# Half of V computed in the opening, half between later attention units

## The chip, the cores and the metric

One core of a Trainium2 chip runs the whole program. The metric is the device time of one execution in microseconds. TensorE (PE) does the matmuls and loads their weights on a parallel path (PEld); VectorE (DVE), ScalarE (ACT) and GpSimd (POOL) do the element-wise work; SyncE (SP) and GpSimd issue most of the transfers.

## What is computed

Forward and backward of a transformer block with modulation, B = 1, S = 2048, D = 512, F = 1792, 32 heads of 16 columns. The change touches only the forward of the attention, cut here from the reference:

```python
mod = (_silu(c) @ w_mod).reshape(c.shape[0], 6, 1, -1)
h = _layernorm(x, axis=-1) * (1 + ca) + sa
qkv = (h @ wqkv).reshape(B, S, 3, H, Dh).transpose(2, 0, 3, 1, 4)
q, k, v = qkv[0], qkv[1], qkv[2]
scores = einsum('bhqd,bhkd->bhqk', q, k) * Dh ** -0.5
o = einsum('bhqk,bhkd->bhqd', softmax(scores), v)
x = x + ga * (o.transpose(0, 2, 1, 3).reshape(B, S, D) @ wo)
```

An MLP with a squared ReLU follows, and the gradients of all of it with respect to nine inputs.

## The kernel before

**Forward attention.** The queries are cut into 4 chunks of 512 (`qc`), the heads into 8 groups of four (`g`), and each group into two halves of two heads (`jp`). A step `n` is one (qc, g, jp); n = 0 to 15 are the first chunk, and pair g is n = 2g and 2g + 1. A step has 16 units, one for each block of 128 keys (`kb`). A unit is: two score matmuls of 512 columns (one for each head), one exponential of 128x1024 on ACT from PSUM to `pu`, and, two or more units later, eight P·V matmuls of 17 columns, which use blocks of `pu` as weights and `Vaug` (V with a column of ones) as the moving operand. Score tiles `st` have two buffers. The score matmul takes all 128 rows: `QTm[j]` holds one head's Q in its 32 rows and zeros elsewhere, and KTq holds the K of the four heads of a group.

**The opening.** `gen_open` loads x, normalises it in four blocks of 512 tokens, transposes and modulates it into `xm1T`, and computes, per block, the K of pair 0 and V (`value`, L517 to L522: four matmuls of 512 columns per 128 tokens, all 32 heads, copied to `Vaug` by DVE or ACT). The first 32 units (n = 0 and 1, exponential L357) run between these pieces: one `next(first)` advances the opening by one piece per unit, so that one unit holds a `value`, or half a block's transposes, or the four matmuls of a Q or K block.

**The background.** From n = 2 on the exponential is L391, and a `Background` object puts other PE work between units. A generator yields after each matmul what it costs (1 for a 512-column projection matmul); each unit grants 1.2 of credit in the first chunk. `gen_qkv` is that generator: for each g from 1 to 7 it waits until the attention is at pair g - 1, then makes, with `gen_fm` (four matmuls, a DVE cast to `ev_fm` or the K tile, a store to `QTq_d` or `KTq_d`), the Q of pair g for the first chunk, then its K in four blocks, then some smaller work (`gen_mod` at g = 2, `gen_vt` at g = 3 to 6, which lets eight units go by while POOL and SP make V's transposes), then the Q of pair g - 1 for the three later chunks. A block that `gen_fm` made is also transposed (L646, on SP) and kept token-major: K's by a POOL store (L648), Q's by a POOL copy (L651) and a POOL store (L653). `ev_fm`, `ev_tm` and `ev_tmc` have three buffers each; the PSUM tile `pps` has two.

**What sets the order.** PE's and SP's instructions are written out by hand in this order. POOL's are placed by the scheduler in the first chunk. Two deadlines force background work: at kb = 5 of the second step of a pair, `bg.until(g + 1)` runs the background until the next pair's Q is done, and `load_q` (L302) loads it into `QTm` through POOL's queue; at the end of that step `bg.until(-(g + 1))` runs it until the next pair's K is done. Work forced so stands in one run on PE, ahead of the next unit's scores. At the end of the first chunk `bg.drain()` finishes the rest, and the tiles of this phase are closed.

```python
for kb in range(ST):
    if kb == (5 if qc == 0 and jp == 1 else 1) and n + 1 < len(order):
        if n < 2 * NQ - 1 and jp == 1:
            bg.until(g + 1)
        load_q(*order[n + 1])
```

Of the kernel before, what the change touches and what calls it, by code (L numbers as in the profile page):

```python
# [10 lines left out]
F32 = mybir.dt.float32  # L11
# [8 lines left out]
P = 128  # L20
DH = 16
# [84 lines left out]
class K:  # L106
# [319 lines left out]
    def gen_open(self, Vaug, KT, QTm, QTo, stp, bg):  # L426

        tc, nc, io = self.tc, self.nc, self.io
        S, D, H, NQ, ST, DT, SC = self.S, self.D, self.H, self.NQ, self.ST, self.DT, self.SC
# [5 lines left out]
        xm1T = self.xm1T = sb.tile([P, DT, S], BF16, name="xm1T")  # L435
        wq = self.wq = sb.tile([P, DT, 3 * D], BF16, name="wqkv")
# [80 lines left out]
        def value(st):  # L517
            pt = ps.tile([P, 512], F32, name="pps")
            for kt in range(DT):
                nc.tensor.matmul(pt[:], lhsT=xm1T[:, kt, st * P:(st + 1) * P], rhs=wq[:, kt, 2 * D:3 * D],  # L520
                                 start=(kt == 0), stop=(kt == DT - 1))
            (nc.scalar.copy if st % 4 == 3 or st in (0, 2) else nc.vector.tensor_copy)(Vaug[:, st, :, 0:DH], pt[:].rearrange("p (h d) -> p h d", d=DH))  # L522

        def pad0(t):
            nc.scalar.copy(self.wpad0[t][:].rearrange("p k (j e) -> p k j e", e=32)[:, :, :, 0:DH],
# [54 lines left out]
        for s4 in range(0, ST, 4):  # L580
# [3 lines left out]
            for k in range(3):  # L584
                value(s4 + k)
                if not last and k in (late, late + 1):
                    norm(n4 + 2 * (k - late))
                    norm(n4 + 2 * (k - late) + 1)
                    if k > late:
                        store(n4)  # L590
                yield 0
            if s4 == 0:
                value(s4 + 3)
                pad(0)
                yield 0
# [3 lines left out]
            if s4:  # L599
                value(s4 + 3)  # L600
                yield 0
# [60 lines left out]
    def gen_qkv(self, kp):  # L662

        nc = self.nc
        S, NQ, ST = self.S, self.NQ, self.ST
        for g in range(1, NQ):
            while self.cur_g < g - 1:
                yield ("wait", 0)
            KT = self.KT_next = kp.tile([P, S], BF16, name="KTq")
            yield from self.gen_fm(self.mps, 0, g, 0)  # L670
            yield (g, 0)
            for s0 in range(0, S, 512):
                yield from self.gen_fm(self.mps, 1, g, s0, dst=KT[:, s0:s0 + 512])
            yield (-g, 0)
            if 3 < g <= 3 + self.DT:
                wt = self.qkv_eb.tile([P, 3 * self.DT, P], BF16, name="wm_t", bufs=1)
                nc.sync.dma_start_transpose(wt[:], w[:])
                nc.gpsimd.dma_start(self.WmT_d[g - 4], wt[:].rearrange("p n k -> p (n k)"))
            if 2 < g < 3 + self.DT:
                w = self.qkv_eb.tile([P, 3 * self.D], BF16, name="wm_s", bufs=2)  # L680
                sc = self.qkv_eb.tile([P, 1], F32, name="wm_c", bufs=2)
                nc.vector.tensor_copy(sc[:], self.opcaT[:, g - 3:g - 2])
                nc.gpsimd.tensor_scalar(w[:], self.wq[:, g - 3, :], sc[:], 1.0, ALU.mult, ALU.mult)
            if g == 2:
                yield from self.gen_mod()
            elif 3 <= g < 3 + self.SC:
                yield from self.gen_vt(4 * (g - 3))
            for s0 in range(512, S, 512):
                yield from self.gen_fm(self.mps, 0, g - 1, s0)
        for s0 in range(512, S, 512):  # L690
            yield from self.gen_fm(self.mps, 0, NQ - 1, s0)

    def gen_vt(self, s0):

        nc = self.nc
        NQ = self.NQ
        vT = self.qkv_eb.tile([P, NQ, 4 * P], BF16, name="vT", bufs=1)
        for k in range(4):
            vp = self.vpads[k]
            v = self.Vaug[:, s0 + k, :, 0:DH].rearrange("p (g j) d -> p g j d", j=4)  # L700
            one = self.qkv_eb.tile([P, 1], F32, name="one", bufs=2)
            nc.vector.memset(one[:], 1.0)
            nc.gpsimd.tensor_scalar(vp[:, :, 0:2, 0:DH], v[:, :, 2:4, :], one[:], 1.0, ALU.mult, ALU.mult)
            nc.gpsimd.tensor_scalar(vp[:, :, 2:4, 0:DH], v[:, :, 0:2, :], one[:], 1.0, ALU.mult, ALU.mult)
            nc.sync.dma_start_transpose(vT[:, :, k * P:(k + 1) * P], vp[:].rearrange("p g j e -> p (g j e)"))
            yield ("wait", 1)
        nc.gpsimd.dma_start(self.VTq_d.rearrange("g p s -> p g s")[:, :, s0 * P:(s0 + 4) * P], vT[:])
# [1258 lines left out]
```

## Time and profile before

| | us |
|---|---|
| median of 3 runs (2507.37 to 2510.71) | 2508.8 |
| the profiled execution's own time | 2500.32 |
| its span | 2498.5 |
| busy in the span: PE, ACT, DVE, POOL | 2410.2, 2283.1, 1695.0, 753.5 |
| opening's units (first exponential L357 to first L391) | 16.73 to 64.19 |
| pairs 1 to 3, first chunk | 64.19 to 153.45 |
| pairs 4 to 6, first chunk | 153.45 to 242.97 |
| pair 7, first chunk | 242.97 to 272.24 |

The profile is of one execution, so its rows add up to its span and not to the median. A row of the page's groups and of the timeline has the line, the engine, the operation, what it writes and reads, the shape, and how many of them (x). In the timeline the first two columns are start and length in microseconds, and a bracket tells how long the engine was idle before it and what ended that. PE's matmuls are pipelined: each row's length includes a fixed delay to its end, so what a matmul costs is read from the distance of the starts. The queue of SP is a row of issues; a long issue is one that was held up.

The granted TensorE clock is 1.00 in every stretch from 0 to 600 us that was looked at.

### The profile page before, as it was taken

The numbers are of one execution on the slowest core, as the hardware profiler recorded it, in microseconds if no ns is written. First come the engines' busy times: TensorE is split into PE (matmuls) and PEld (weight loads), VectorE is DVE, ScalarE is ACT, GpSimd is POOL, SyncE is SP. The second block draws the span as 40 slices with busy tenths as digits, with TensorE's granted clock in tenths as the row PEclk, the third lists the DMA queues.
The fourth block names the chain that finished last, engine by engine and source line by source line (L and its number), as shares of the span: only waits on it lengthen the run. The fifth ranks groups of instructions, "written<-read, shape, count | busy, mean of one in ns | idle before, by whom it ended". The sixth has DMA issues, their size and how long they took to land.

```text
span 2498.5 us, 67897 instructions
## 1 busy us (share of the span) xinstructions
PE 2410.2 (96%) x26211; PEld 1061.6 (42%) x26439; DVE 1695.0 (68%) x3487; ACT 2283.1 (91%) x3757; POOL 753.5 (30%) x1337
## 2 busy tenths in 40 slices
PE   8999999999999999999999999999999999999998
PEld 4555555555555555583233332333333333333343
DVE  6222322422332343576999999999999999999957
ACT  7999999999999997534999999999999999999945
POOL 2344531220131022245222323322333222322223
PEclk9999999999999999999999999999999999999999
DMA  4589661541243045499999999999999999999997
GB/s 166 135 179 208 169 125 47 132 100 40 92 114 98 23 123 147 110 199 216 232 235 233 232 227 231 237 234 231 230 235 239 234 230 236 234 233 236 238 217 192
DMA packets 1293547, 454.13 MB, mean 182 GB/s; under 512 B 1236948, under 2 KB 1261398, under 8 KB 1293222
## 3 DMA queue, kind: packets, MB, share of 16 engines
q1 hardware_dynamic: 1252422, 344.68, 71.8%
q0 software_dynamic: 38720, 104.04, 13.9%
q8 instruction: 207, 3.39, 0.6%
q10 hardware_dynamic: 2080, 1.05, 0.2%
q14 instruction: 118, 0.97, 0.1%
HBM read 75.83 MB, written 64.49 MB: 56 GB/s over the span
## 4 chain that ended last, share of the span: by engine, by line
PE 49%; ACT 35%; DMA 7%; issue 5%; DVE 3%; POOL 1%; SPq 1%; ACTq 0%; DVEq 0%; POOLq 0%
ACT pu L391 26%; PE st L1608 17%; PE acckv L1459 8%; ACT pu L1611 6%; DMA dsT<-ds 5%; PE accq L1484 5%; PE st L388 4%; PE dp L1522 2%; PE accbank L322 2%; PE dps L1050 2%; PE dp L1659 1%; PE st L1754 1%; ACT csq L1540 1%; PE pps L1237 1%; DVE ds L1526 1%
## 5 line engine op out<-in xcount | busy, mean ns | idle before, releaser
L1526 DVE TENSOR_TENSOR ds<-dp,pu 128x512 bf16<-128x512 f32 x1888 | 1166.0, 682 | 34.6 <-PE dp L1522 19.1
L1611 ACT ACTIVATE pu<-st 128x512 bf16<-128x512 f32 x2048 | 1073.8, 666 | 34.7 <-PE st L1608 21.3
L391 ACT ACTIVATE pu<-st 128x1024 bf16<-128x1024 f32 x992 | 912.1, 1077 | 4.2 <-PE st L388 3.7
L388 PE MATMUL st<-QTm,KTq 128*128 128x512 bf16 x1859 | 560.9, 377 | 27.1 <-ACT pu L391 6.1
L322 PEld LDWEIGHTS <-pu 128*128 128x128 bf16 x8192 | 346.7, 96 | 236.1 <-issue 3.0
L1522 PE MATMUL dp<-kvm,q 64*128 64x512 bf16 x1024 | 365.0, 384 | 2.0 <-DVE ds L1526 0.7
L322 PE MATMUL accbank<-Vaug,pu 128*128 128x17 bf16 x8192 | 357.4, 171 | 8.3 <-ACT Vaug L522 1.1
L1522 PE MATMUL dp<-kvm,dOTg 64*128 64x512 bf16 x1024 | 363.6, 383 | 0.3
L1608 PE MATMUL st<-kvm,q 64*128 64x512 bf16 x1024 | 349.4, 382 | 5.4 <-ACT pu L1611 0.2
L1608 PE MATMUL st<-kvm,QTg 64*128 64x512 bf16 x1024 | 348.1, 381 | 6.5
L1541 POOL TENSOR_TENSOR ds<-csq,pu 128x512 bf16<-128x512 f32 x128 | 147.2, 1150 | 627.0 <-ACT csq L1540 553.6
L388 PEld LDWEIGHTS <-KTq 128*128 128x128 bf16 x1984 | 188.4, 96 | 176.9 <-issue 124.8
L1459 PE MATMUL acckv<-ds,Qg 128*16 128x512 bf16 x1024 | 176.2, 382 | 0.3
L1459 PE MATMUL acckv<-pu,q 128*16 128x512 bf16 x1024 | 176.3, 383 | 0.0
L1459 PE MATMUL acckv<-ds,q 128*16 128x512 bf16 x1024 | 176.2, 383 | 0.0
L1459 PE MATMUL acckv<-pu,dOg 128*16 128x512 bf16 x1024 | 176.0, 382 | 0.0
L302 POOL DMA_DIRECT2D QTm<-QTq_d x124 | 63.1, 511 | 341.5 <-PE st L388 320.0
L1608 PEld LDWEIGHTS <-q 64*128 64x128 bf16 x1024 | 67.0, 94 | 163.5 <-issue 150.6
L1608 PEld LDWEIGHTS <-QTg 64*128 64x128 bf16 x1024 | 67.1, 94 | 160.6 <-issue 145.7
L329 DVE RECIPROCAL rl<-accbank 128x4 f32<-128x4 f32 x128 | 22.9, 179 | 158.3 <-PE accbank L322 158.2
L1522 PEld LDWEIGHTS <-q 64*128 64x128 bf16 x1024 | 88.8, 93 | 52.9 <-issue 43.3
L1522 PEld LDWEIGHTS <-dOTg 64*128 64x128 bf16 x1024 | 88.2, 93 | 52.9 <-issue 43.8
(390 smaller groups left out, 3055.1 us busy)
## 6 DMA issues: line engine op xcount, KB each, us to landing
KTq<-KTq_d POOLq DMA_DIRECT2D x24, 512.0 KB, 3.9
duT_d<-auT POOLq DMA_DIRECT2D x3, 1792.0 KB, 7.9
aT_d<-rT POOLq DMA_DIRECT2D x3, 1792.0 KB, 11.5
KTq_d<-KTq SPq DMA_DIRECT2D x32, 128.0 KB, 2.1
QTq_d<-ev_fm SPq DMA_DIRECT2D x32, 128.0 KB, 4.3
ktm_d<-ev_tm POOLq DMA_DIRECT2D x32, 128.0 KB, 2.5
VTq_d<-vT POOLq DMA_DIRECT2D x4, 1024.0 KB, 6.3
dx<-dx_d SPq DMA_DIRECT2D x16, 256.0 KB, 4.6
```

What stands on the lines that cost most here:

```text
L302: nc.gpsimd.dma_start(QTm[j][32 * j:32 * j + 32, :], self.QTq_d[g, 32 * j:32 * j + 32, 512 * qc:512 * (qc + 1)])
L322: nc.tensor.matmul(acc[:, a, sub, :], lhsT=pu[:, a, sub * P:(sub + 1) * P], rhs=Vaug[:, kb, h, :], start=(kb == 0 and a == 0 and sub == 0) ...
L388: nc.tensor.matmul(stt[:, a, :], lhsT=KT[:, kb * P:(kb + 1) * P], rhs=QTm[2 * jp + a][:], start=True, stop=True)
L391: nc.scalar.activation(pu[:], stt[:], ACT.Exp, scale=self.scale)
L1050: nc.tensor.matmul(pt[:], lhsT=a[st], rhs=g_tm[:, st, :], start=(st == 0), stop=(st == ST - 1))
L1459: nc.tensor.matmul(acckv[r:r + DH, :], lhsT=T[n][:, ib, col:col + DH], rhs=src[:, a, :], start=(ib == 0), stop=(ib == ST - 1))
L1484: nc.tensor.matmul(accq[r:r + 32, o:o + 256], lhsT=T["K"][:, 4 * c + sub, col:col + 32], rhs=v[:, r // 32 % 2 * 2:r // 32 % 2 * 2 + 2, 4 * ...
L1522: nc.tensor.matmul(dp[:], lhsT=T["dOT"][rd, ib * P:(ib + 1) * P], rhs=masked["VT"][a][rd, 512 * c:512 * (c + 1)], start=True, stop=True)
L1526: nc.vector.tensor_tensor(dsg[:, i, a], dp[:], pu[:, a, :], ALU.mult)
L1541: nc.gpsimd.tensor_tensor(dsg[:, i, 1], f[:], pu[:, 1, :], ALU.mult)
L1608: nc.tensor.matmul(stt[:], lhsT=T["QT"][rs, q], rhs=masked["KT"][a][rs, c0:c0 + 512], start=True, stop=True)
L1611: nc.scalar.activation(pu[:, a, :], stt[:], ACT.Exp, scale=self.scale)
```

## The change

`value` computes the first 256 columns of V only, that is heads 0 to 15 (pairs 0 to 3). A new generator `gen_v` computes the other 256 in the background, for token blocks 0 to 3 after the K of pair 1, 4 to 9 after that of pair 2, and 10 to 15 after that of pair 3; its matmuls cost 0.55 of credit each. The Q of the later chunks of pairs 0, 1 and 2 is no longer made at g = 1, 2, 3 but at g = 4, 5, 6, ahead of that of pairs 3, 4 and 5. After g = 7 nothing differs.

```diff
         def value(st):
             pt = ps.tile([P, 512], F32, name="pps")
             for kt in range(DT):
-                nc.tensor.matmul(pt[:], lhsT=xm1T[:, kt, st * P:(st + 1) * P], rhs=wq[:, kt, 2 * D:3 * D],
+                nc.tensor.matmul(pt[:, :D // 2], lhsT=xm1T[:, kt, st * P:(st + 1) * P], rhs=wq[:, kt, 2 * D:2 * D + D // 2],
                                  start=(kt == 0), stop=(kt == DT - 1))
-            (nc.scalar.copy if st % 4 == 3 or st in (0, 2) else nc.vector.tensor_copy)(Vaug[:, st, :, 0:DH], pt[:].rearrange("p (h d) -> p h d", d=DH))
+            (nc.scalar.copy if st % 4 == 3 or st in (0, 2) else nc.vector.tensor_copy)(
+                Vaug[:, st, 0:H // 2, 0:DH], pt[:, :D // 2].rearrange("p (h d) -> p h d", d=DH))
...
             if g == 2:
                 yield from self.gen_mod()
-            elif 3 <= g < 3 + self.SC:
+            if g < 4:
+                yield from self.gen_v((0, 4, 10, ST)[g - 1], (0, 4, 10, ST)[g])
+            if 3 <= g < 3 + self.SC:
                 yield from self.gen_vt(4 * (g - 3))
-            for s0 in range(512, S, 512):
-                yield from self.gen_fm(self.mps, 0, g - 1, s0)
+            for gq in [q for q in (g - 4, g - 1) if g > 3 and (q < 3) == (q == g - 4)]:
+                for s0 in range(512, S, 512):
+                    yield from self.gen_fm(self.mps, 0, gq, s0)
         for s0 in range(512, S, 512):
             yield from self.gen_fm(self.mps, 0, NQ - 1, s0)
+
+    def gen_v(self, a, b):
+
+        nc, D, H, DT = self.nc, self.D, self.H, self.DT
+        for st in range(a, b):
+            pt = self.mps.tile([P, 512], F32, name="pps")
+            for kt in range(DT):
+                nc.tensor.matmul(pt[:, :D // 2], lhsT=self.xm1T[:, kt, st * P:(st + 1) * P],
+                                 rhs=self.wq[:, kt, 2 * D + D // 2:3 * D], start=(kt == 0), stop=(kt == DT - 1))
+                if kt < DT - 1:
+                    yield 0.55
+            nc.vector.tensor_copy(self.Vaug[:, st, H // 2:, 0:DH], pt[:, :D // 2].rearrange("p (h d) -> p h d", d=DH))
+            yield 0.55
```

## The prediction

> **What bounds the kernel now.** I read the busy time by stage first, then the timelines of TensorE (PE) and ScalarE (ACT) in the opening, then those of the DMA queues of SyncE (SP) and GpSimd (POOL). The change touches the opening and the first query chunk. The stretches below are the opening's 32 attention units, pairs 1 to 3 (n = 2 to 7), and pairs 4, 5, 6 and 7. The columns: stretch, length, then busy time and instructions of PE, PEld, DVE, ACT, POOL, the clock, the DMA share.
>
> ```profile
> core 0: us, PE busy (x) PEld busy (x) DVE busy (x) ACT busy (x) POOL busy (x), PEclk, DMA share, GB/s
> 16.73:64.19 47.46, 44.20 (x435) 24.23 (x442) 31.22 (x68) 38.73 (x45) 14.24 (x24) 1.00 0.33 113
> 64.19:153.45 89.26, 86.20 (x1076) 49.38 (x1093) 23.39 (x62) 88.54 (x97) 35.24 (x69) 1.00 0.63 147
> 153.45:183.49 30.04, 28.20 (x350) 16.32 (x356) 7.27 (x25) 29.58 (x34) 13.88 (x26) 1.00 0.87 188
> 183.49:213.24 29.75, 28.12 (x352) 16.27 (x355) 6.84 (x21) 29.52 (x32) 14.23 (x27) 1.00 0.91 201
> 213.24:242.97 29.73, 28.10 (x352) 16.23 (x355) 7.08 (x22) 29.52 (x32) 15.39 (x29) 1.00 0.87 201
> 242.97:272.24 29.27, 27.29 (x349) 15.98 (x352) 5.85 (x17) 29.27 (x33) 12.55 (x24) 1.00 0.73 185
> ```
>
> ACT has 8.7 us to spare in the opening and almost none after it: there the exponentials set the pace, 0.915 us apart (pair 7: 29.27 us for 32). The DMA share is already 0.87 to 0.91 in pairs 4 to 6.
>
> In the opening PE is the pacer of most units:
>
> ```profile
> 29.73 0.35 PE L322 MATMUL accbank<-Vaug,pu 128*128 128x17 bf16 x8
> 29.94 0.59 PE L354 MATMUL st<-QTo,KTq 128*128 128x512 bf16 x2
> 30.37 1.03 PE L520 MATMUL pps<-wqkv,xm1T 128*128 128x512 bf16 x4
> 31.23 0.35 PE L322 MATMUL accbank<-Vaug,pu 128*128 128x17 bf16 x8
> 30.63 1.02 ACT L357 ACTIVATE pu<-st 128x1024 bf16<-128x1024 f32 x1 [0.47 <-PE st L354]
> ```
>
> Starts give the real cost: 8 P·V matmuls 0.21 us, 2 score matmuls 0.43, 4 V matmuls 0.86 (0.214 each); together 1.497, and ACT idles 0.47 before each exponential.
>
> What several background matmuls in one unit cost after the opening is seen where the schedule forces three:
>
> ```profile
> 211.67 0.38 PE L322 MATMUL accbank<-Vaug,pu 128*128 128x17 bf16 x9
> 211.91 0.81 PE L631 MATMUL pps<-xm1T,wpad 128*128 128x512 bf16 x3
> 212.55 0.59 PE L388 MATMUL st<-QTm,KTq 128*128 128x512 bf16 x2
> 213.24 1.94 ACT L391 ACTIVATE pu<-st 128x1024 bf16<-128x1024 f32 x2 [0.23 <-PE st L388]
> ```
>
> That exponential starts 1.267 us after the last, 0.35 over the pace: 0.24 + 3 x 0.214 + 0.43 = 1.31 on PE is all but the whole of it. PE has no lead.
>
> Last, the queue that every Q and K block passes, a store and then a transpose on SP, in pair 5, and the POOL queue that loads the next Q behind it:
>
> ```profile
> 188.55 6.85 SPq L705 DMA_TRANSPOSE vT<-vpad  x4
> 195.82 0.48 SPq L642 DMA_DIRECT2D QTq_d<-ev_fm  x1
> 196.41 1.21 SPq L646 DMA_TRANSPOSE ev_tm<-ev_fm  x1
> ...
> 204.04 0.53 SPq L642 DMA_DIRECT2D QTq_d<-ev_fm  x1
> ```
>
> ```profile
> 206.91 0.54 POOL L653 DMA_DIRECT2D qtm_d<-ev_tmc  x1 [0.30 <-POOL ev_tmc L651]
> 207.44 1.01 POOL L302 DMA_DIRECT2D QTm<-QTq_d  x2
> ```
>
> Three late Q blocks take 8.2 us of SP (195.82 to 204.04) before the store of the next pair's own Q, and only behind their three token-major copies (L651) does POOL load that Q.
>
> **The change part by part.**
> *Removed from the opening.* 64 V matmuls go from 512 to 256 columns. No V matmul of 256 stands in the trace; the nearest rows are 0.214 us at 512 and 0.056 at 128 (8 transposes of L504 start within 0.45 us), so I take 0.107: 6.8 us of PE, the bound from above. What of it shows, unit by unit: units 0 to 3 nothing, since the next block's normalisation holds PE (POOL's rstd at 19.61 us waits for DVE's statistics, not for V, and PE waits at 23.03 for the result). Units 8 to 10, 24 to 26 and 29 are paced by PE at 1.497: 7 x 0.427 = 3.0. Units 16 to 18 end in transposes that wait 0.51 for DVE: two casts of 0.69 and four normalisations stand in line there, the casts fall to an estimated 0.43 (0.17, as DVE's smallest instructions take, and half the rest), and with the earlier V the line ends some 0.9 earlier. Units 13 and 21 are paced by ACT; its copy of 0.60 loses about 0.18 each: 0.36. Sum 4.3, from below 3.2 if a short matmul exposes its weight load.
>
> The Trainium skill's "TensorE: Matmul & The Clock Gate", section "Back-to-back issue gap", gives a sustained spacing of 81 ns at 128 columns and 131 at 512 for streams with weight loads. By it a matmul would lose only about 33 ns (estimate, on a straight line between the two) and the opening 2.1 us of PE instead of 6.8; the rows above say 56 and 214, so the measurement decides.
>
> *Added in pairs 1 to 3.* The same 64 matmuls, two to a unit in the built order, take 0.214 in place of one projection matmul's 0.214. A unit then needs 0.24 + 0.43 + 0.21 = 0.88 against 0.915, so nothing; without that cover it would be 6.8. 16 casts of about 0.43 on DVE, which is busy 23.4 of 89.26 there: nothing. The copies of the later Q blocks leave these pairs.
>
> *Moved into pairs 4 to 6.* Nine Q blocks (pairs 0, 1, 2; three each), one pair's three into each of pairs 4, 5, 6. Per pair: 12 matmuls, 3 casts, 3 stores and 3 transposes on SP, 3 POOL copies (0.41) and 3 POOL store issues (0.54). The background schedule grants 1.2 matmuls a unit, 38 in a pair; a pair's demand goes to 4 + 16 + 24 = 44 and four vT steps hold it for 8 units. So the forced completion before the load of the next pair's Q (kb 5 of n = 9, 11, 13) finds work left. The built order of PE shows it: 12 projection matmuls in a row at each of these places, where before there was one or two, and 4 instead of 3 at the end of each pair. Price from the forced three: 0.35 + 9 x 0.214 = 2.27, three times 6.8; and 3 x 0.214 = 0.6 for the fours. 7.4 in all; from below 6.0, if an exponential in hand covers a fifth.
>
> *The next Q's load.* In the order built for POOL it stands behind six copies, not three, and its data behind six blocks on SP. Pair 4: vT ends on SP at 165.1; SP passes a block in 1.93 us (store 0.53, transpose 1.20, gaps) to 2.74 (8.22 / 3). With 2.3 six are through at 178.9, and the next Q's store starts at 179.0. Such stores landed a median 4.8 and at most 7.0 us after their start in pairs 4 to 6: 183.8 to 186.0; from the first load's issue to the second's landing it was 2.8 (180.16 to 182.97): 186.6 to 188.8. The second scores need it at 182.8 + 2.4 of delay = 185.2. That is 1.4 to 3.6 late, against 0.4 before (PEld waits 0.36 at 183.02): 1.0 to 3.2. I take 2.0. In pairs 5 and 6 the load had 1 to 2 us to spare (issued 207.44 and 237.96, needed near 213.0 and 242.7) and PE comes later itself, so 1.0 each. Sum 4.0; from 0 to 9 (three times 3). Late next: the first scores of n = 10, 12, 14, hence ACT.
>
> The DMA page of the skill ("DMA: Bandwidth & Descriptors", "Latency and other measured facts") has 261 GB/s for a DMA transpose; by that 128 KB would be 0.5 us (estimate) and nine of them 4.5 us. SP's own rows, 1.2 us or more each, are longer.
>
> Sum: -4.3 + 7.4 + 4.0 = +7.1. The profiled execution took 2500.3 us (span 2498.5, 1.8 around it) and would take 2507.4; the runs' median stands 8.5 above it, so 2508.8 + 7.1 = 2515.9.
>
> **The rivals.**
> *Only the forced runs cost* (loads in time): -4.3 + 7.4 = +3.1, 2511.9. For it: two of three loads had time to spare, and a forced run gives the load 2.3 more. Against: six blocks ahead of it instead of three.
> *SP becomes the bound of pairs 4 to 6.* Its queue idles about 3.5 us in pair 5's 29.75 (2.5 of it before 219.17), so 26.3 + 3 x 2.74 = 34.5 a pair, 4.75 too long: 14.2, with one late landing of 2 more 16.2; less 4.3, +11.9, 2520.7. For it: DMA share 0.9, and the three ev_fm buffers are free only after a transpose has landed, so casts, then PSUM, then PE stand behind SP. Against: in pair 4 SP still starts with no backlog.
> *The runs of twelve are hidden, and it is not slower*: -4.3 alone, 2504.5. The place is kb 5 of n = 9, 11, 13; it needs exponentials in hand for 2.3 us, and decides from the point where a boundary costs less than 1.4 in all. Against: score buffers are two, and a run of three already shows 0.35.
>
> **How the numbers follow.** Forecast (2512.5 to 2521) 0.50, only the runs 0.25, SP bound 0.15, hidden 0.10. The likeliest gives 2515.9. The range takes the first two and most of the third: 2509.5 to 2522.5. A change under 0.2% (5.0 us) can't be told from none. Slower by more (2513.8): 0.45 of the forecast, 0.05 of the second, all of the third, 0.65. Faster by more: 0.03, the hidden case with an opening above 5. The same: the rest, 0.32.
>
> **What would show it.** Right: the opening's 32 units end near 60 us instead of 64.19; three gaps of 3.2 us between exponentials at kb 4 to 5 of n = 9, 11, 13; more idle ACT at the starts of n = 10, 12, 14, ended by scores that wait for the load of QTm; pairs 4 to 6 at 32 to 36 us each instead of 29.8; everything from pair 7 on as long as before. Wrong: value units still 1.4 us apart (matmuls of 256 not at half price); the gaps missing; PE waiting on casts in pairs 4 to 6 (SP the bound); or a stall in pairs 1 to 3, where I have put nothing.

## The result, and the profile after

Eleven executions of each kernel: before 2512.05 us median (2502.66 to 2523.86), after 2524.93 (2516.64 to 2534.28). The ratio is 1.0061, 95% interval 1.0042 to 1.0080, so the change costs 15.3 us (10.6 to 20.1) of 2512 (the two medians alone differ by 12.9). The forecast was slower by 7.1, to 2515.9, with 2509.5 to 2522.5 as its range: the side is right, the size is about half, and the median lies outside the range. Of the 9.0 us between 2515.9 and 2524.93, 3.3 is the base: the forecast started from 2508.8, the median of three runs. The same kernel's times spread over some 20 us, wider than the effect, while the forward's stages repeat within 0.4 us where two kernels have the same order of work, and mostly within 0.1. From here on I compare stages.

The stretches of the kernel after, as they were shown of before (opening, pairs 1 to 3, then pairs 4, 5, 6 and 7; same columns):

```profile
core 0: us, PE busy (x) PEld busy (x) DVE busy (x) ACT busy (x) POOL busy (x), PEclk, DMA share, GB/s
16.73:60.16 43.43, 38.67 (x437) 24.18 (x443) 28.77 (x68) 37.43 (x45) 14.27 (x24) 1.00 0.35 122
60.16:149.05 88.89, 85.67 (x1101) 52.12 (x1120) 23.85 (x72) 88.49 (x98) 26.22 (x50) 1.00 0.50 115
149.05:184.39 35.34, 30.88 (x366) 17.50 (x369) 8.79 (x21) 29.72 (x34) 17.83 (x35) 1.00 0.88 187
184.39:221.67 37.28, 32.22 (x363) 17.84 (x367) 9.15 (x25) 29.91 (x32) 17.62 (x34) 0.95 0.90 186
221.67:259.86 38.19, 32.09 (x364) 17.79 (x368) 9.16 (x25) 29.87 (x33) 17.71 (x34) 0.96 0.83 182
259.86:289.12 29.26, 27.32 (x348) 15.98 (x352) 5.95 (x17) 29.26 (x32) 11.66 (x23) 1.00 0.74 171
```

The opening gained 4.04 us (47.46 to 43.42), pairs 1 to 3 are 0.38 shorter (no more than the same work differs by: 88.87 in e9 below, 89.27 in before), pair 7 is the same, and pairs 4 to 6 went from 89.52 to 110.81: +21.29. ACT's work in them is the 29.7 to 29.9 it was; what grew is its idle time. At the end of the first chunk the kernel is 16.9 behind. Chunk 3 adds 3.1 (one stall, below) and the others return 0.9, so the forward ends 19.05 later. The rest of the gap of 24.6 between the two profiled executions lies in the backward, which no edit here touches and which took between 1519 us (before, the shortest of all) and 1543 in the eleven executions profiled: that part is not explained by the change.

The opening's units that hold a V piece, in the timeline of after:

```profile
29.94 0.60 PE L520 MATMUL pps<-wqkv,xm1T 128*128 128x256 bf16 x4
30.38 0.35 PE L322 MATMUL accbank<-Vaug,pu 128*128 128x17 bf16 x8
30.58 0.59 PE L354 MATMUL st<-QTo,KTq 128*128 128x512 bf16 x2
31.01 0.60 PE L520 MATMUL pps<-wqkv,xm1T 128*128 128x256 bf16 x4
```

From one group of L520 to the next it is 1.07 us, where it was 1.497: 0.107 us a matmul of 256 columns, half of 0.214, as the prediction took it.

What ended the idle time in pairs 4 to 6 (columns: the waiting engine and tile, the releaser, us in all, times, longest):

```profile
PE pps L632 <- DVE ev_fm L639: 10.8, 4, 3.5
PE st L388 <- ACT pu L391: 2.8, 9, 0.3
...
DVE ev_fm L639 <- DMA ev_tm<-ev_fm: 14.6, 5, 4.5
...
ACT pu L391 <- PE st L388: 21.3, 12, 4.0
```

It is a chain. ACT waits for scores, PE for a PSUM tile that DVE has not emptied, DVE for an `ev_fm` buffer whose transpose has not landed. In the stretch of before the first and third of these lines did not occur, and ACT's wait was 0.9 in all. No wait of PE for the load of `QTm` is left, where the prediction put 4.0 us. In the timeline of pair 5 (kb 4 to 7 of n = 11; start, length; rows of PEld and POOL left out):

```profile
202.67 2.83 PE L632 MATMUL pps<-xm1T,wpad 128*128 128x512 bf16 x11
202.73 1.97 SPq L647 DMA_TRANSPOSE ev_tm<-ev_fm  x1
203.73 0.69 DVE L639 CAST ev_fm<-pps 128x512 bf16<-128x512 f32 x1 [0.58 <-PE pps L632]
204.80 1.41 SPq L643 DMA_DIRECT2D QTq_d<-ev_fm  x1
205.34 0.59 PE L388 MATMUL st<-QTm,KTq 128*128 128x512 bf16 x2
205.77 0.38 PE L322 MATMUL accbank<-Vaug,pu 128*128 128x17 bf16 x9
206.03 1.02 ACT L391 ACTIVATE pu<-st 128x1024 bf16<-128x1024 f32 x1 [2.29 <-PE st L388]
206.31 1.45 SPq L647 DMA_TRANSPOSE ev_tm<-ev_fm  x1
...
208.91 0.69 DVE L639 CAST ev_fm<-pps 128x512 bf16<-128x512 f32 x1 [4.49 <-DMA ev_tm<-ev_fm]
209.66 0.38 PE L632 MATMUL pps<-xm1T,wpad 128*128 128x512 bf16 x1 [3.51 <-DVE ev_fm L639]
...
210.69 1.02 ACT L391 ACTIVATE pu<-st 128x1024 bf16<-128x1024 f32 x1 [3.64 <-PE st L388]
```

The forced run is there at 202.67: ACT idles 2.29 behind it, the gap the prediction had. Then comes a second one that it had not. PE made its blocks in a burst, faster than SP carries them off. The next block's first matmul needs a PSUM tile, the tile needs a cast, and the cast has had no free buffer for 4.49 us; PE stands 3.51, and the scores behind that matmul with it. In gaps between exponentials, 0.92 and 0.99 before: 3.33, 3.33 and 4.40 for the runs of n = 9, 11 and 13, and 3.93, 4.67 and 5.05 right behind.

### The profile page after: what moved, and what is told of

Its sections match the earlier page's. It is cut to its first block, busy times and chain, and to the rows that moved or that the text cites. A ratio compares the mean times of both kernels' runs of the same rounds, so it can differ in the third digit from the quotient of the medians.

```text
span 2523.2 us, 68049 instructions
## 1 busy us (share of the span) xinstructions
PE 2421.2 (96%) x26273; PEld 1068.6 (42%) x26503; DVE 1703.6 (68%) x3503; ACT 2283.4 (90%) x3757; POOL 754.4 (30%) x1337
## 3 DMA queue, kind: packets, MB, share of 16 engines
q0 software_dynamic: 38720, 104.04, 13.6%
## 4 chain that ended last, share of the span: by engine, by line
PE 50%; ACT 32%; DMA 9%; issue 5%; DVE 2%; POOL 1%; DVEq 0%; ACTq 0%; SPq 0%; POOLq 0%
ACT pu L391 25%; PE st L1625 16%; PE acckv L1476 8%; DMA dsT<-ds 7%; ACT pu L1628 5%; PE accq L1501 5%; PE st L388 4%; PE accbank L322 2%; PE dp L1539 2%; PE dps L1067 2%; PE st L1771 1%; PE dp L1676 1%; PE pps L1254 1%; DVE ds L1543 1%; DMA ev_tm<-ev_fm 1%
## 5 line engine op out<-in xcount | busy, mean ns | idle before, releaser
L1501 PE MATMUL accq<-dsT,keep 128*32 128x256 bf16 x1632 | 104.6, 278 | 5.3 <-DMA dsT<-ds 5.2
```

Of the source, the lines that this page charges most:

```text
L1501: nc.tensor.matmul(accq[r:r + 32, o:o + 256], lhsT=T["K"][:, 4 * c + sub, col:col + 32], rhs=v[:, r // 32 % 2 * 2:r // 32 % 2 * 2 + 2, 4 * ...
```

## The experiments

Theory at the start: the forced runs cost what was predicted, and the rest is the queue on SP, made dearer by the three `ev_fm` buffers. The rival: the split of V costs in pairs 4 to 6 in some way, or the load of `QTm` does. Each is one profiled execution unless a ratio is given.

**e1 and e2: one half of the change each.** e1 keeps the whole V in the opening, with idle steps of the same credit where `gen_v` stood, and moves Q:

```diff
+                nc.tensor.matmul(pt[:], ... rhs=wq[:, kt, 2 * D:3 * D],
...
-                yield from self.gen_v((0, 4, 10, ST)[g - 1], (0, 4, 10, ST)[g])
+                for _ in range(4 * ((4, 6, 6)[g - 1])):
+                    yield 0.55
```

> V whole in the opening as before; only the nine later Q blocks of pairs 0 to 2 are moved to pairs 4 to 6, and the background keeps its credit in pairs 1 to 3 by idle yields. Theory (the moved Q blocks make the loss: twelve projection matmuls forced in one run, then casts that wait for one of three ev_fm buffers): opening 47.5 us as before, pairs 4 to 6 at 35.3, 37.3 and 38.2 us within 1 us each, as in the changed kernel, so 20 to 22 us longer than before. Rival (the V matmuls and casts in the background cost it): pairs 4 to 6 within 2 us of 29.8 each.

Measured: opening 47.46, pairs 1 to 3 88.85, pairs 4 to 6 33.52, 34.28 and 37.44, together 105.24, pair 7 29.26. The Q move by itself makes 15.7 of the 21.3, with the same two kinds of gap (4.52 and 4.54 at the runs of n = 9 and 11, 3.33 then 4.85 at that of n = 13). That is short of the 20 to 22 expected: pairs 4 and 5 lie 1.8 and 3.0 us under their figures. Why after has 5.6 us more was not found; that the background stands at other places when each run starts, and meets SP's queue otherwise, is a guess.

e2 splits V and leaves Q where it was:

```diff
-            for gq in [q for q in (g - 4, g - 1) if g > 3 and (q < 3) == (q == g - 4)]:
-                for s0 in range(512, S, 512):
-                    yield from self.gen_fm(self.mps, 0, gq, s0)
+            for s0 in range(512, S, 512):
+                yield from self.gen_fm(self.mps, 0, g - 1, s0)
```

> V split as in the changed kernel, the later Q blocks where they were. Theory (a run of forced projection matmuls costs 0.214 us each and then the wait for ev_fm): opening 43.4 us, pairs 4 to 6 as before (29.7 to 30.0 us each), and the two forced runs that the built order now has in pairs 2 and 3 (15 and 14 matmuls at kb 4 to 5 of n = 5 and 7) cost 2.9 and 2.7 us by their length plus 2 to 4 us each for ev_fm, so pairs 1 to 3 at 98 to 103 us instead of 89.3. Rival (half of V is free in the background): pairs 1 to 3 at 89 to 91 us.

Measured: opening 43.42, pairs 1 to 3 98.05 (+8.8), pairs 4 to 6 90.97 (+1.5). So Q was in the way: with both in pairs 1 to 3, PE is busy 95.15 of 98.05 us, and forced runs of 15 and 14 matmuls leave gaps of 3.98 and 3.56 between exponentials at kb 5 of n = 5 and 7: 3.06 and 2.64 over the pace, near the 2.9 and 2.7 expected for their length. The wait for `ev_fm` expected behind them leaves no second gap. Neither half of the change is the good one: pairs 1 to 6 grow by 10.2 in e2 (for 4.0 gained in the opening), by 15.3 in e1, by 20.9 in after.

**e3: six `ev_fm` buffers.** After, with

```diff
-            ev = eb.tile([P, 512], BF16, name="ev_fm")
+            ev = eb.tile([P, 512], BF16, name="ev_fm", bufs=6)
```

> The changed kernel with six ev_fm buffers instead of three. Theory (PE stands behind casts that wait for a free ev_fm buffer): the second gap after each forced run (3.9, 4.7 and 5.1 us between exponentials, and the half-clock units after the last two) is gone, the first stays at 3.3; pairs 4 to 6 at 32 to 33 us each, 97 in all instead of 111. Rival (SP's queue is the bound whatever the buffers): the wait moves to the first scores of n = 10, 12 and 14, and the three pairs still take 105 us or more.

Measured: 32.32, 34.87 and 35.96, together 103.16; pair 7 30.47. The second gaps are gone (0.92 where they were 3.93 and 4.67), and the wait of PE for casts too. But of the 13.6 us that stand behind the runs (worked out under e6b) only 7.65 came back, 6.4 with the longer pair 7, and 103.16 meets neither the theory's 97 nor the rival's 105. PE's waits in the stretch:

```profile
PE st L388 <- DMA QTm<-QTq_d: 4.7, 3, 2.2
PE st L388 <- ACT pu L391: 2.2, 7, 0.3
```

The gaps between exponentials at the starts of n = 12 and 14 became 4.08 and 4.44: the late load that the prediction had, and which in after the casts hid by making PE later than the load. At the start of n = 10 nothing is late (1.47). So the theory and the rival are the same queue seen at two places.

**e9: nothing but SP.** The kernel before, its computation unchanged, with three more stores and transposes a pair that nobody reads:

```diff
+                if 4 <= g < NQ - 1:
+                    dup = self.qkv_eb.tile([P, 4, P], BF16, name="dup", bufs=3)
+                    nc.sync.dma_start(self.scr_d[:, :], KT[:, s0:s0 + 512])
+                    nc.sync.dma_start_transpose(dup[:], KT[:, s0:s0 + 512])
                 yield from self.gen_fm(self.mps, 0, g - 1, s0)
```

> The kernel before with the whole V in the opening and no Q block moved; only SP gets more in pairs 4, 5 and 6: ahead of each pair's three later Q blocks one store (of a piece of K that is there already, to a scratch buffer) and one transpose into a tile that nothing reads. PE, DVE and POOL get nothing more. Theory, SP's queue is full in pairs 4 to 6: it issues for some 26 us of the 29.7 there and each block of store and transpose takes 2 to 2.7 us, so three more make 32 to 34 us a pair; pairs 4, 5 and 6 each grow by 2 to 5 us (95.5 to 104 together, from 89.5), and the new idle time ends in PE waiting for the load of QTm, or in casts that wait for an ev_fm buffer (a transpose that has not landed). Rival, SP has room and only the runs of matmuls on PE matter: each of these pairs stays within 1 us of before (29.8), 89 to 92 together. Opening 47.5, pairs 1 to 3 89.3 and pair 7 29.3 in both.

Pairs 4, 5, 6 and 7, and PE's first wait in them (its lines are one higher than before's from the first edit on):

```profile
153.07:186.29 33.22, 28.37 (x350) 16.24 (x356) 7.30 (x25) 29.58 (x33) 12.83 (x24) 1.00 0.94 188
186.29:221.21 34.92, 29.63 (x352) 16.50 (x356) 7.08 (x21) 29.81 (x32) 14.71 (x28) 0.94 0.88 192
221.21:256.42 35.21, 29.37 (x353) 16.40 (x356) 7.01 (x18) 29.73 (x32) 15.16 (x28) 0.94 0.87 192
256.42:287.79 31.37, 29.25 (x349) 16.58 (x353) 5.62 (x16) 29.59 (x32) 13.35 (x26) 0.92 0.78 177
```

```profile
PE st L389 <- DMA QTm<-QTq_d: 10.7, 5, 4.3
PE st L389 <- ACT pu L392: 2.4, 8, 0.3
```

103.35 in pairs 4 to 6, inside the theory's 95.5 to 104: +13.83, with not one matmul, cast or POOL operation added (PE has 350, 352 and 353 instructions, before 350, 352 and 352). The gaps at the starts of n = 10, 12 and 14 are 4.69, 5.06 and 6.17, before 1.50, 1.27 and 1.26. Load `QTm` in the timeline of e9, at the start of n = 12:

```profile
217.58 1.01 POOL L303 DMA_DIRECT2D QTm<-QTq_d  x2
...
219.74 0.39 PE L389 MATMUL st<-QTm,KTq 128*128 128x512 bf16 x1 [2.84 <-DMA QTm<-QTq_d]
220.53 0.59 PE L389 MATMUL st<-QTm,KTq 128*128 128x512 bf16 x1 [0.41 <-DMA QTm<-QTq_d]
...
221.22 1.02 ACT L392 ACTIVATE pu<-st 128x1024 bf16<-128x1024 f32 x1 [4.02 <-PE st L389]
```

POOL issues it at 217.58, 31.3 us after the pair's start at 186.29; in before it went at 207.44, 24.0 after 183.49. So it stands 7.3 later in a pair whose scores wait for it. Nine blocks carry 13.8 us, 1.5 a block: the rival, that SP has room, is out. Whether the room that lacks is SP's issue or the DMA engines behind it (share 0.87 to 0.94) this kernel can't tell, since it loads both.

**e6 and e6b: the next pair's own Q ahead of the late blocks.** e3, with Q's block for the next pair made before the later chunks':

```diff
-            yield from self.gen_fm(self.mps, 0, g, 0)
-            yield (g, 0)
+            if g < 5:
+                yield from self.gen_fm(self.mps, 0, g, 0)
+                yield (g, 0)
...
+            if 4 <= g < NQ - 1:
+                yield from self.gen_fm(self.mps, 0, g + 1, 0)
+                yield (g + 1, 0)
```

In e6 (and e7) pairs 5 to 7 of the first chunk read the K of the pair before them; e6b takes each pair's own K and computes all of the reference.

> The changed kernel with six ev_fm buffers, and in pairs 4 to 6 the next pair's own Q block made before the six later ones, so that its store stands first behind vT on SP and its load ahead of five of the copies on POOL. The lack of background credit is the same, so the built order now has runs of 15 projection matmuls at the end of pairs 4, 5 and 6 and none at kb 5. Theory (three separate costs: the length of the forced runs, the ev_fm buffers, the late load of the next Q): only the length is left, 0.35 + 12 x 0.214 = 2.9 us a pair instead of 0.35 to 0.6, so 32 to 32.5 us for each of pairs 4 to 6, 97 in all, and no wait for QTm at n = 10, 12, 14. Rival (SP's queue sets the length of a pair whatever is first in it): 103 or more in all, as with six buffers alone, with waits for some other transfer.

> As e6 (six ev_fm buffers, and for pairs 5 to 7 the next pair's own first Q block made ahead of the late Q blocks), with each pair reading its own K, so that the whole computation is done. Theory, the load of the next Q has to stand ahead of the late blocks and the casts need free buffers: pairs 4 to 6 take 96 to 99 us together (after 110.8, six buffers alone 103.2), no wait for QTm at the starts of n = 10, 12 and 14. Rival, that the gain of e6 came from pairs 5 to 7 not waiting for their own K: 102 to 108. In time against the kernel before: the forward's first chunk keeps +3 to +5 (opening -4, pairs 4 to 6 +7.5), and the stall behind late weights at the start of the second chunk, 12 us in e6, stays: slower by 12 to 20 us in the forward.

Measured, both: 32.45, 32.37 and 32.35, together 97.17. The stages of e6b:

```profile
149.05:181.50 32.45, 30.80 (x366) 17.51 (x369) 8.88 (x21) 29.56 (x34) 16.97 (x33) 1.00 0.88 187
181.50:213.87 32.37, 30.71 (x363) 17.45 (x367) 9.16 (x25) 29.47 (x33) 14.56 (x28) 1.00 0.93 198
213.87:246.22 32.35, 30.74 (x364) 17.41 (x367) 9.15 (x25) 29.46 (x33) 16.70 (x32) 1.00 0.92 207
```

Both met their theory. These are three equal pairs with the same matmuls as after (366, 363 and 364 instructions), the same blocks for SP to carry in the chunk, and a DMA share as high. Nothing waits for `QTm` or a cast there; one gap of 3.93 is left at the end of each pair, the late blocks forced in one run before the next K. So 7.65 of the 21.29 is the runs on PE, and the other 13.64, the waits behind SP's queue, is gone from these pairs: six buffers gave back 7.65 of it (e3; that the figure is the same is chance), the order the other 5.99.

It is not gone from the forward. SP begins V's transposes (vT, once a pair) later and later in e6b, and PE waits in the next chunk:

```profile
152.68 6.91 SPq L727 DMA_TRANSPOSE vT<-vpad  x4
...
189.79 8.09 SPq L727 DMA_TRANSPOSE vT<-vpad  x4
...
224.73 7.45 SPq L727 DMA_TRANSPOSE vT<-vpad  x4
...
278.86 0.39 SPq L1123 DMA_DIRECT2D wo<-in_A_wo_dram  x1
...
296.23 0.61 PE L388 MATMUL st<-QTm,KTq 128*128 128x512 bf16 x1 [6.91 <-DMA QTm<-QTq_d]
```

These vT stand 3.6, 8.3 and 10.9 us behind the starts of their pairs, in before 4.4, 5.1 and 5.9. From the second to the third SP takes 34.9 (34.5 and 34.7 in e9, 30.7 and 30.6 in before), while PE's pairs take 32.4: the queue falls behind. SP issues the first load for chunk 2 (`wo`) 3.4 us after that chunk's start at 275.48, in before 3.8 ahead of it; POOL waits 5.8 for it (5.3 in before) and only then loads `QTm` (284.30). The second chunk takes 245.61 against 237.08 in before and 236.85 in after, with a gap of 9.40 between exponentials at the start of n = 17 (13.19 in e6), where PE waits 8.0 for `QTm`. So 8.8 of the 13.64 is lost again, and the forward of e6b ends 5.0 us before that of after and 14.1 after that of before. e6b was also timed: 2526.82 us (10 runs), ratio 1.0054 to before, interval 1.0035 to 1.0073. It does not beat before, and its time cannot be told from that of after.

**e4, e7, e8: attempts at a better version.** e4 deals the later Q blocks out (2 at g = 1, then 4, 4, 4 and 10 at g = 4 to 7) and lets V's transposes hold nothing up; e7 is e6 without that hold; e8 moves only token blocks 8 to 15 of V's second half, with a flatter deal of Q and six buffers:

```diff
+            for _ in range((0, 2, 0, 0, 4, 4, 4, 10)[g]):
+                yield from self.gen_fm(self.mps, 0, *late.pop(0))
...
-            yield ("wait", 1)
+            yield ("wait", 0)
```

> V split (token blocks 0 to 4, 5 to 8, 9 to 15 at g = 1, 2, 3); the 24 later Q blocks in order, 2 at g = 1, 4 each at g = 4, 5, 6, the last 10 after that; gen_vt no longer lets eight units go by. The built order has no run over 3 projection matmuls. Theory (the loss is the forced runs and the buffers behind them): opening 43.4 us, pairs 1 to 7 within 1 us of before each, span 3 to 4.5 us shorter than before. Rival (SP's queue is the bound): pairs 4 to 6 at 32 us or more each, since a pair has one block more on SP.

> As e6_own_q_first, and gen_vt no longer lets eight units go by, which gives the background 9.6 of credit a pair more: runs of 6, 10 and 10 matmuls are left at the ends of pairs 4, 5 and 6. Theory: 0.9, 1.8 and 1.8 us for the runs, pairs 4 to 6 at 93 to 95 us in all. Rival (SP's queue is the bound): projection matmuls come while SP still works on vT, casts wait or loads are late, and the three pairs take 98 or more.

> Only token blocks 8 to 15 of V's second half are moved to the background (2, 3, 3 at g = 1, 2, 3); blocks 0 to 7 are computed whole in the opening. Six ev_fm buffers, no units let go by in gen_vt, later Q blocks spread 2, 2, 2, 3, 4, 4, 7. The built order has no run over 3 matmuls. Theory: opening 44.7 us (value units 16 to 18, 21, 24 to 26 and 29 are shorter, 2.7 us), pairs 1 to 7 within 1 us of before in all, so the last exponential of the forward comes 1.5 to 3 us earlier than before's, which a span would hardly show. Rival (SP's queue is the bound, one more block a pair is too many): pairs 4 to 6 at 91 us or more in all, and no gain.

| us | before | after | e4 | e7 | e8 |
|---|---|---|---|---|---|
| opening | 47.46 | 43.42 | 43.43 | 43.43 | 45.76 |
| pairs 4 to 6 | 89.52 | 110.81 | 95.07 | 95.35 | 94.60 |
| chunk 2 | 237.08 | 236.85 | 245.16 | 248.93 | 244.92 |
| SP's load of `wo`, from chunk 2's start | -3.8 | -2.6 | 12.2 | 3.0 | 0.5 |

e4 missed its theory (5.6 over before instead of 3 at most) and came near the rival's 32 us a pair in two pairs of three (31.99, 32.26, 30.82); e7 met its 93 to 95 but for 0.35; e8's opening was 1 us over its forecast and its pairs went to the rival. All have a new stall of 7 to 11 us at the start of chunk 2, where PE waits for transfers that land late (6.5 us in e4 and 10.2 in e7 on a transpose of the first chunk's O). SP's first load for chunk 2 comes after that chunk's start in all three, as in e6 (5.5) and e6b (3.4); in before, after, e1, e2, e3 and e9, which have no such stall, it comes 2.5 to 4.6 us ahead of it. That this is the cause is argued from these times, not tried. One-run times: e1 2527.7, e2 2522.2, e3 2522.7, e4 2525.1 (before beside them 2517.5), e6 2530.8, e7 2538.2, e8 2526.1 (before 2515.9), e9 2527.4 (before 2507.8, 13 runs). None beats before: its forward ends at 979.48, the earliest of the others, e2's, at 987.77. The most that this split could gain is the opening's 4.0 us, 0.16%.

## Why the prediction was half right

*The opening, -4.3.* Measured -4.04, and unit by unit as it was added up: the seven units paced by PE lost 0.43 each (the last 0.32), units 16 to 18 0.83 net, units 13 and 21 0.21 each, and what units 0 to 3 gained was gone at unit 4. The price of a short matmul from the rows at 512 and 128 columns held. By the spacing that the Trainium skill gives for streams with weight loads ("TensorE: Matmul & The Clock Gate", section "Back-to-back issue gap") PE would have saved 2.1 us at most (an estimate), half of what was gained. The run sides with that section's formula for a single matmul, columns / 2.4 + 2.5 ns: 109 ns at 256 columns (an estimate by it), against 107 measured.

*Pairs 1 to 3 at nothing, and everything from pair 7 on as before.* -0.38, and 0.00 in pair 7: held, but for chunk 3 (below). e2 shows that the cover was real and thin: with Q kept, these pairs grow by 8.8, where 6.8 was named for V matmuls without cover.

*Forced runs, 6.8, and fours, 0.6.* The run's own gaps are 3.33, 3.33 and, with 1.1 of a cast in it, 4.40: three times 2.41 is 7.2. The fours cost 0.2 each in pairs 5 and 6. e6b has 7.65 for all of it. This term held, and the rival that hides the runs is out.

*The next Q's load, 4.0 with 9 at most: the step that failed.* The sum charged SP's longer queue only through this load. It gave nothing to casts that wait for one of the three `ev_fm` buffers, though the third rival names these buffers, and PE waiting on casts stands among the signs of being wrong. In after it is the casts: what stands behind the runs costs 13.64 (the second gaps are 3.0, 3.8 and 4.1 over the pace, 1.1 is in the first gap of n = 13, most of the rest is the slow clock of the last section), and PE is then so late that the load is in time. With six buffers the load itself shows: 0.0, 2.8 and 3.2 us over before's gaps at the starts of n = 10, 12 and 14, together 6.0, where the sum had 2.0, 1.0 and 1.0. So the larger cost was missing, and this term was two thirds of its size, with the most put on the pair that lost nothing. e9, which has no runs to hide them, has late loads of 3.2, 3.8 and 4.9 (4.69 less 1.50, and so on) and 1.9 of smaller ones. Why they grow from pair to pair is not shown; a backlog handed on explains little of it, since SP begins vT only 0.6, 1.2 and 0.1 us later behind the start of its pair in e9 than in before. A reading under the term was off too: 4.8 is the median landing with a store of pair 7 among them; for pairs 4 to 6 the trace has three, 3.7, 5.9 and 7.0.

*The rivals.* "SP becomes the bound" had this mechanism, chain and all, at 14.2 for the three pairs (13.64 behind the runs in after, 13.8 in e9), and 0.15 of the chance. Its 34.5 us a pair is what SP takes from one vT to the next in e9. It was weighed against the forecast as if the two excluded each other, and its sum left the forced runs out. In after both are paid: -4.3 + 7.4 + 14.2 = +17.3, against 16.9 at the end of the first chunk and 15.3 by the ratio. That they add up so well is in part luck: in e3, with the same runs and the same blocks, both together cost 13.64, since the delay by a run hides part of a late load. The reason given against it, that SP starts pair 4 without a backlog, fits the smaller loss in pair 4 (5.3, then 7.5 and 8.5).

*Open.* Chunk 3's stall: one gap of 3.44 at unit 579 and a slow one after it, 3.1 us, with PE waiting for a transpose of the normalised input. It goes with the split of V: 3.0 to 3.4 in e2, e3, e6 and e6b and 2.6 in e4 and e7, but 1.1 as before in e1 and e9, where the opening is whole, and in e8, where it is whole for token blocks 0 to 7. Why is not known. And the backward's wander, which hides which part of these 3 us the total keeps.

## What to carry to other kernels

A block of work is not its matmuls: list every queue it passes, and price each queue by its slack in the stretch that the block moves to; here a move that left the columns of PE's matmuls the same cost 7.65 us on PE and 13.6 behind SP's queue. A ring of few buffers is part of that price, since it carries the queue's delay back to PE. When two resources both run short, their costs are terms of one sum, not rivals, unless the same idle time pays for both, as in part it did in e3. When a move must be made, put what the next step needs ahead of what may be late: with buffers enough, that took the 13.6 out of these pairs. It did not make the queue faster: 8.8 came back in the next chunk, so look where the queue's backlog is paid.

## What the hardware showed besides

After a long wait the matmuls were slow. In after PE idled 3.51 us until 209.66, and the granted clock was 0.5 for 3.41 us from 210.2; the same came at 247.7, behind the stall of pair 6, and in the idle of 2.91 us in pair 4 it did not. Two windows of after (columns as in the stretches above):

```profile
210.00:212.00 2.00, 2.00 (x17) 0.88 (x15) 0.53 (x1) 1.02 (x1) 1.42 (x4) 0.55 0.70 168
212.00:214.00 2.00, 2.00 (x19) 0.95 (x18) 0.00 (x0) 1.29 (x2) 0.54 (x1) 0.60 1.15 97
```

With PE full and the clock at 0.55 to 0.60, units take 1.52 us in place of 0.92, so each such stall costs 0.6 to 1.2 more than its length; before, the forward has none.

The Trainium skill ("TensorE: Matmul & The Clock Gate", section "Part 1: The HAM clock gate (the "warmup" mystery)") has the clock halve after an idle window of 3413 ns, and these windows run freely. The length and the free running agree: the three slow stretches in the forward of after start at 210.20, 247.74 and 589.08, the later two 11 and 111 times 3.413 us after the first, and last 3.41 each; in e9 they start at 186.18, 220.31 and 254.45, 10 and 20 times 3.413 after the first. That the window has to be idle does not: in the 3.41 us ahead of the three starts of after PE's rows leave 2.87, 3.25 and 1.82 idle. The 2.91 of pair 4 fell into two such windows, 1.78 and 1.20, and the clock stayed at 1.00. No single threshold shows in these runs: 1.51 idle in a window brought the slow clock in e3 (at 217.38), 1.89 in before (317.12 to 320.53) did not.
